# Where VectorE's side work stands in a queue: halves of x and slices of w_out behind the next subtraction, an earlier read-back, one fence a visit

## The chip, the cores and the metric

The kernel runs on one core of one Trainium2 chip. Its time is the device time of one execution in microseconds (us); the time before is the median of three runs. A profile of one execution gives the spans of the engines: TensorE (PE: matmuls; PEld: its weight loads), VectorE (DVE), ScalarE (ACT), GpSimd (POOL) and SyncE (SP), which issues most of the DMA transfers.

## What is computed

Two blocks, one after the other. The first is a retention layer: a state per batch and head decays and takes in the outer product of k and v at every step, and q reads it. The second is a feed-forward layer with SiLU.

```python
# 4 batches, 8 heads, 768 steps, head size 64
for t in range(S):
    state = gamma * state + einsum('bhd,bhe->bhde', k[:, :, t], v[:, :, t])
    y[:, :, t] = scale * einsum('bhd,bhde->bhe', q[:, :, t], state)
x = y.transpose(0, 2, 1, 3).reshape(3072, 512)
h = x @ w_in                       # 512 -> 2048
g = h * (1 / (1 + exp(-h)))
out = g @ w_out                    # 2048 -> 512
```

q, k and v are float32, the weights are given as float64.

## The kernel before

The steps are worked in chunks of 128. A unit is one chunk of one batch: 6 chunks by 4 batches, 24 units. Four units with the same chunk make a group c, and give 512 columns of x. A **visit** m runs three units in a pipeline: it transposes k and q of unit m, makes the scores of unit m-1 and the output y of unit m-2. TensorE's order is that of the program text; on the other engines a scheduler orders the instructions, when the program is built, and `tc.issue_after(i)` keeps an instruction behind instruction i.

```python
    def visit(m):
        first, mid, last = (0 <= m - i < len(units) for i in range(3))
        if first:
            stage_t(m)                       # transposes of k and q, copied by ScalarE to kt and qt
        if last:
            scores, states_with, yp = stage_y(m - 2)
            scores()                         # y from the masked scores
        if mid:
            sc, sums = score_tile(m - 1)
            stage_s(m - 1, sums)
        if last:
            states_with(0)                   # y from the states, part 0
        if mid:
            stage_a(m - 1, sc)
            with tc.issue_after(taken_out[0]) if taken_out else ExitStack():
                finish_a(m - 1, sc, sums)    # VectorE: mask, mid, state
            scale_q(m - 1)
        # ... (constants in visit 0)
        if first:
            scale_k(m)
        if last:
            states_with(1)                   # part 1
            finish_y(m - 2, yp)              # y becomes x
        # ... (loads of later k, q, v)
```

Matrix products of float32 are made of three products of parts: x is split into a high part, a low part and a mixture, and so are the weights. y lies in the PSUM tile `yp`, of which there is one, until the low half is taken:

```python
    def split_x(c, b, y, raw):
        # ... xh, xl: views of xt[c] for block b
        held[:] = [nc.scalar.activation(out=xh, in_=y, func=AF.Copy, scale=HALF).ins]
        nc.vector.tensor_tensor(out=xl, in0=y, in1=xh.bitcast(FP32), op=ALU.subtract)
        nc.vector.scalar_tensor_tensor(out=x[2], in0=x[1].bitcast(FP32), scalar=-1.0 / EPS,
                                       in1=x[0].bitcast(FP32), op0=ALU.mult, op1=ALU.add)

    LATE = 2

    def late_x(b):
        if b == 0:
            xt[LATE] = xpool.tile([128, 3, KIN, NT], FP32R, tag="xt", name=f"xt_{LATE}")
        y = hpool.tile([128, KIN, C], FP32, tag="hs", name=f"yr_{b}")
        nc.sync.dma_start(out=y, in_=y_dram[b])
        split_x(LATE, b, None, y)
```

The x of group 2 is made once into the place of the last four w_in slices, and a second time, from y kept in DRAM, for its last four products (`late_x`).

A **product** (c, f) is 12 matmuls of 128x512: eight into the PSUM bank `ha`, four into `hb`. ScalarE copies ha, VectorE subtracts hb, ScalarE applies SiLU, and g goes to DRAM. `turn` hands out three banks in rotation, to ha, hb and the transposed k of a visit.

```python
    def turn(name):
        turns[0] += 1
        return ps_h.tile([128, 512], FP32, tag=f"h{turns[0] % 3}", name=name)

    def product_in(c, f):
        ha, hb = turn(f"ha_{c}_{f}"), turn(f"hb_{c}_{f}")
        for i in range(3):
            for kk in range(KIN):
                nc.tensor.matmul(hb if i == 2 else ha, ...)
        hs = hpool.tile([128, NT], FP32, tag="hs", name=f"g_{c}_{f}")
        nc.scalar.activation(out=hs, in_=ha, func=AF.Copy, scale=ONE_E)
        taken_out[:] = [nc.vector.tensor_tensor(out=hs, in0=hs, in1=hb, op=ALU.subtract).ins]
        nc.scalar.activation(out=hs, in_=hs, func=AF.Silu)
        pending.append((c, f, hs))
```

The weights come as float64 and are turned into float32, a slice of 128 rows or columns at a time: one operation on ScalarE and six on VectorE (`convert_w`, called by `take_w`). A slice of w_in is then split into its three parts; a slice of w_out is stored in DRAM and read and split in group 5 (`w_out`). The result `cw` of a slice of w_out has one buffer.

```python
        with tc.issue_after(evac[0]) if evac else ExitStack():
            nc.scalar.activation(out=a.bitcast(FP32), in_=hi.bitcast(FP32), func=AF.Abs, scale=65536.0)
        nc.vector.tensor_scalar(out=s, ...)              # cs, L194
        nc.vector.tensor_scalar(out=a.bitcast(FP32), ...)  # ca, L196
        nc.vector.scalar_tensor_tensor(out=s, ...)       # cs, L199
        nc.vector.tensor_scalar(out=p, ...)              # cp, L201
        nc.vector.scalar_tensor_tensor(out=p.bitcast(FP32), ...)  # cp, L203
        nc.vector.tensor_tensor(out=w, ...)              # cw, L206
```

The order of the products, where a slice is taken, and which visit stands behind which product:

```python
    pairs = [(c, f) for f in range(4) for c in range(2)]
    three = [x for f in range(4, half) for x in ((0, f), (1, f), (2, f - 4))]
    rest = ([(2, f) for f in range(half - 4, NF - 4)] +
            [(c, f) for c in range(2) for f in range(half, NF - 4)])
    last = [(c, f) for c in range(3) for f in range(NF - 4, NF)]
    groups = [(c, f) for c in range(3, NC) for f in range(NF)]
    steps = pairs + three + rest + last + groups          # NF = 16, half = 8, NC = 6
    # takes: see the diff
    behind = {(1, f): lambda f=f: visit(EARLY + 2 + f) for f in range(4)}   # EARLY = 8
    at = ([(1, NF - 1)] + [(2, f) for f in range(NF - 4, NF - 1)] +
          [(c, 4 * i + 1) for c in range(3, NC - 1) for i in range(B)])
    for i, x in enumerate(at):
        behind[x] = lambda m=EARLY + 6 + i: visit(m)
```

A fence is a small memset on GpSimd that waits for one matmul and is waited for by another. It stands twice in a visit, ahead of each part of the states, because matmuls on different rows of the array would otherwise add to one PSUM bank at the same time.

Of the kernel before, what the change touches and what calls it, by code (L numbers as in the profile page):

```python
# [25 lines left out]
EPS = 2.0 ** -12  # L26
HALF = 1.0 - 2.0 ** -13
ONE_E = 1.0 + EPS
# [3 lines left out]
def kernel(  # L32
# [40 lines left out]
    scale = 1.0 / math.sqrt(D)  # L73
# [12 lines left out]
    one = pool("one", 1)  # L86
# [60 lines left out]

    staged = {}  # L150

    def load_w(i):
        if i >= 2 * NF:
            return
        if wide:
            t = stage.tile([128, 2 * DM], U32, tag="wf", name=f"wf_{i}")
            w_in, w_out, n = moe_w_in.bitcast(U32), moe_w_out.bitcast(U32), 256
        else:
            t = stage.tile([128, DM], FP32, tag="wf", name=f"wf_{i}")
            w_in, w_out, n = moe_w_in, moe_w_out, 128  # L160
        if i < NF:
            to = t.rearrange("p (i o f) -> o p i f", o=2, f=n)
            src = w_in[:, ts(i, n)].rearrange("(i o p) f -> o p i f", o=2, p=128)
            nc.sync.dma_start(out=to[0], in_=src[0])
            for j in range(2):
                nc.sync.dma_start(out=to[1, ts(j, D)], in_=src[1, ts(1 - j, D)])
        else:
            nc.sync.dma_start(out=t, in_=w_out[ts(i - NF, 128), :])
        staged[i] = t

    def convert_w(i):

        if i + W_AHEAD not in staged:
            load_w(i + W_AHEAD)
        t = staged.pop(i)
        if not wide:
            return t
        words = t.rearrange("p (c w) -> p c w", w=2)
        lo, hi = words[:, :, 0], words[:, :, 1]
        a = conv.tile([128, DM], U32, tag="ca", name=f"ca_{i}")
        s = conv.tile([128, DM], U32, tag="cs", name=f"cs_{i}")
        p = conv.tile([128, DM], U32, tag="cp", name=f"cp_{i}")  # L190
        with tc.issue_after(evac[0]) if evac else ExitStack():
            nc.scalar.activation(out=a.bitcast(FP32), in_=hi.bitcast(FP32), func=AF.Abs,
                                 scale=65536.0)
        nc.vector.tensor_scalar(out=s, in0=hi, scalar1=0x80000000, scalar2=None,  # L194
                                op0=ALU.bitwise_and)
        nc.vector.tensor_scalar(out=a.bitcast(FP32), in0=a.bitcast(FP32),  # L196
                                scalar1=bits(1024 << 20), scalar2=bits((1279 << 20) - 1),
                                op0=ALU.max, op1=ALU.min)
# [7 lines left out]
        nc.vector.tensor_tensor(out=w, in0=s.bitcast(FP32), in1=p.bitcast(FP32), op=ALU.add)  # L206
        return w
# [1 line left out]
    evac, held, w_sb = [], [], {}  # L209
    taken = [0]  # L210

    def take_w(between=lambda: None):
        i = taken[0]
        taken[0] += 1
        if i >= 2 * NF:
            return
        w32 = convert_w(i)
        between()
        if i < NF:
            w_sb[i] = split_w(i, w32, "wi", scale)  # L220
        else:
            nc.sync.dma_start(out=wo_dram[i - NF], in_=w32)
# [56 lines left out]


    xt, kt, qt, am = {}, {}, {}, {}
    taken_out = []
    state, steps_of = {}, {}


# [91 lines left out]
    def stage_y(n):  # L377

        vs, amn, qtn = kqv["v"].pop(n), am.pop(n), qt.pop(n)
        states = steps_of.pop(n)  # L380
        yp = banks("y", f"y_{n}")[:, :, : 4 * D].rearrange("p o (a t) -> p o a t", a=HP)

        started, done, new = set(), [], []

        def product(a, o, j, lhsT, rhs):
            e = j ^ (a % 2)
            i = nc.tensor.matmul(yp[ts(e, D), o, a, :], lhsT=lhsT, rhs=rhs,  # L387
                                 start=(e, o) not in started, stop=True,
                                 skip_group_check=True).ins
# [12 lines left out]
        def states_with(part):  # L402
            new.append(part)
            for a in range(HP):
                o = part ^ (a % 2)
                for j in range(2):
                    if states[o] is not None:
                        product(a, o, j, states[o][ts(j, D), a, :], qtn[ts(j, D), a, ts(o, D)])

        return scores, states_with, yp  # L410
# [15 lines left out]
    def split_x(c, b, y, raw):  # L426
        x = [xt[c][:, i, :, ts(b, C)] for i in range(3)]
        if raw is None:
            xh, xl = (t.rearrange("p a (o t) -> p o a t", o=2) for t in x[:2])
        else:  # L430
            (xh, xl), y = x[:2], raw
        held[:] = [nc.scalar.activation(out=xh, in_=y, func=AF.Copy, scale=HALF).ins]
        nc.vector.tensor_tensor(out=xl, in0=y, in1=xh.bitcast(FP32), op=ALU.subtract)  # L433
        nc.vector.scalar_tensor_tensor(out=x[2], in0=x[1].bitcast(FP32), scalar=-1.0 / EPS,
                                       in1=x[0].bitcast(FP32), op0=ALU.mult, op1=ALU.add)

    LATE = 2

    def late_x(b):
        if b == 0:
            xt[LATE] = xpool.tile([128, 3, KIN, NT], FP32R, tag="xt", name=f"xt_{LATE}")
        y = hpool.tile([128, KIN, C], FP32, tag="hs", name=f"yr_{b}")
        nc.sync.dma_start(out=y, in_=y_dram[b])
        split_x(LATE, b, None, y)

    def visit(m):

# [35 lines left out]
                nc.tensor.matmul(hb if i == 2 else ha, lhsT=w_sb[f][:, i, ts(kk, 128)],  # L485
                                 rhs=xt[c][:, i, kk, :], start=kk == 0 and i != 1,
                                 stop=kk == KIN - 1 and i != 0)
        hs = hpool.tile([128, NT], FP32, tag="hs", name=f"g_{c}_{f}")
        nc.scalar.activation(out=hs, in_=ha, func=AF.Copy, scale=ONE_E)  # L489
        taken_out[:] = [nc.vector.tensor_tensor(out=hs, in0=hs, in1=hb, op=ALU.subtract).ins]  # L490
        nc.scalar.activation(out=hs, in_=hs, func=AF.Silu)  # L491
        pending.append((c, f, hs))

# [64 lines left out]
    groups = [(c, f) for c in range(3, NC) for f in range(NF)]  # L558
    steps = pairs + three + rest + last + groups
    takes = [(0, f) for f in range(half)]  # L560
    takes += [(2, half), (2, half + 1)]
    takes += [(0, half), (0, half + 2), (1, half), (1, half + 2)]
    takes += [x for x in (last + groups)[::3]][:NF]
    behind = {(1, f): lambda f=f: visit(EARLY + 2 + f) for f in range(4)}
    at = ([(1, NF - 1)] + [(2, f) for f in range(NF - 4, NF - 1)] +
          [(c, 4 * i + 1) for c in range(3, NC - 1) for i in range(B)])
    for i, x in enumerate(at):
        behind[x] = lambda m=EARLY + 6 + i: visit(m)
    for i, bs in enumerate(((0, 1), (2,), (3,))):
        behind[1, NF - 4 + i] = lambda bs=bs: [late_x(b) for b in bs]  # L570
    for n, (c, f) in enumerate(steps):
        product_in(c, f)
        if (c, f) in takes:
            take_w()
        put_g(1)
        behind.get((c, f), lambda: None)()
        if c == NC - 1:
            if f == 0:
                get_w(0)
                get_w(1)  # L580
            if f < NF - 4:
# [68 lines left out]
```

## Time and profile before

| | |
|---|---|
| time, median of 3 runs (range) | 659.12 us (659.02 to 660.37) |
| span of the profiled execution | 655.4 us, granted TensorE clock 0.988 |
| busy: TensorE, its weight loads | 617.1 us (94%), 509.2 us (78%) |
| busy: VectorE, ScalarE, GpSimd | 428.5 us (65%), 288.1 us (44%), 14.9 us (2%) |

The busy time by stage, in us:

| stage | from to | TensorE | VectorE | ScalarE |
|---|---|---|---|---|
| visits 0 to 9, first slices of w_in | 0 to 55 | 37.3 | 38.4 | 28.5 |
| first ten products, visits 10 to 13 | 55 to 104 | 43.3 | 44.5 | 28.9 |
| products of groups 0 to 2, no visit | 104 to 186 | 82.0 | 67.5 | 53.7 |
| products with visits 14 to 25 | 186 to 339 | 143.3 | 110.7 | 71.4 |
| rest of the products with w_in | 339 to 388 | 49.0 | 33.8 | 36.4 |
| products with w_out | 388 to 655 | 262.2 | 133.7 | 69.2 |

Matmuls overlap each other, so a busy TensorE may still be slower than at its best; gaps are read from the start times in the timeline. Line numbers such as L490 are those of the kernel before; a DVE line "g<-g,hb" is the subtraction of a product.

### The profile page before, as it was taken

The page shows a single profiled execution, that of the slowest core. Times are in us where ns is not written, and L with a number is a line of the kernel's source. Part 1 is how long each engine was busy: PE and PEld are TensorE (multiplying, and loading weights), DVE is VectorE, ACT ScalarE, POOL GpSimd, SP SyncE. Part 2 cuts the span into 40 slices and gives each one's busy share as a digit, 9 for nine tenths or more (in the row PEclk, how much of TensorE's full clock was granted, in tenths as well). Part 3 has the DMA queues.
Part 4 walks back from the last instruction along what each step waited for, and adds up shares of the span by engine and source line. Part 5 has one row for each costly group of instructions (what it writes and reads, how often), then busy time and mean ns, then how long its engine had stood idle before and what let it go on. Part 6 is the DMA issues. An engine that isn't in the chain of part 4 may idle for free.

```text
span 655.4 us, 13531 instructions
## 1 busy us (share of the span) xinstructions
PE 617.1 (94%) x5440; PEld 509.2 (78%) x5440; DVE 428.5 (65%) x736; ACT 288.1 (44%) x522; POOL 14.9 (2%) x94
## 2 busy tenths in 40 slices
PE   4788889999999899999989999999999999999996
PEld 3676777888877687888768888888888888888885
DVE  2898989967968867658948856545463645454631
ACT  4546566756645444454437972222231412222311
POOL 3100000000000000000000000000000000000000
PEclk9998989999999999999999999999999999999999
DMA  9996775553577866767736654343242433433301
GB/s 196 211 209 153 198 199 179 185 171 127 192 242 170 235 178 162 226 170 237 240 113 225 202 169 127 100 159 101 92 163 95 147 110 98 159 99 95 129 0 64
DMA packets 123070, 103.64 MB, mean 158 GB/s; under 512 B 80000, under 2 KB 88192, under 8 KB 123008
## 3 DMA queue, kind: packets, MB, share of 16 engines
q1 hardware_dynamic: 119552, 96.49, 50.9%
q10 hardware_dynamic: 3456, 6.29, 2.6%
q8 instruction: 42, 0.69, 0.5%
q14 instruction: 20, 0.16, 0.1%
HBM read 66.06 MB, written 36.70 MB: 157 GB/s over the span
## 4 chain that ended last, share of the span: by engine, by line
PE 70%; DVE 17%; ACT 4%; DMA 3%; issue 3%; SPq 2%; ACTq 0%; DVEq 0%; POOL 0%; POOLq 0%
PE ha L485 18%; PE hb L485 9%; PE ob L612 7%; PE o L610 7%; PE oa L610 7%; PE o L611 7%; PE o L612 7%; PE oa L611 7%; SPq L144 2%; DVE cp L203 2%; DVE g L490 2%; DVE xt L433 2%; DVE cs L199 2%; PE y L387 1%; DVE am L363 1%
## 5 line engine op out<-in xcount | busy, mean ns | idle before, releaser
L485 PE MATMUL ha<-xt,wi 128*128 128x512 f32 x768 | 194.2, 395 | 6.0 <-DVE g L490 4.3
L485 PEld LDWEIGHTS ha<-xt,wi 128*128 128x128 f32 x768 | 142.6, 188 | 40.3 <-DVE g L490 8.3
L536 DVE TENSOR_TENSOR gs<-gr,gs 128x512 fp32r<-128x512 f32 x96 | 62.1, 685 | 90.3 <-ACT gs L534 90.3
L534 ACT ACTIVATE gs<-gr 128x512 fp32r<-128x512 f32 x96 | 53.5, 621 | 134.2 <-issue 131.8
L485 PE MATMUL hb<-xt,wi 128*128 128x512 f32 x384 | 103.0, 390 | 1.2 <-ACT g L489 1.1
L491 ACT ACTIVATE g<-g 128x512 f32<-128x512 f32 x96 | 60.6, 631 | 78.4 <-DVE g L490 78.2
L490 DVE TENSOR_TENSOR g<-g,hb 128x512 f32<-128x512 f32 x96 | 65.5, 682 | 44.4 <-PE hb L485 33.8
L485 PEld LDWEIGHTS hb<-xt,wi 128*128 128x128 f32 x384 | 71.9, 188 | 17.1 <-ACT g L489 1.6
L612 PE MATMUL ob<-wo,gs 128*128 128x512 f32 x192 | 75.3, 392 | 0.0
L610 PE MATMUL o<-wo,gs 128*128 128x512 f32 x192 | 74.7, 389 | 0.0
L610 PE MATMUL oa<-wo,gs 128*128 128x512 f32 x192 | 74.7, 389 | 0.0
L611 PE MATMUL o<-wo,gs 128*128 128x512 f32 x192 | 74.7, 389 | 0.0
L612 PE MATMUL o<-wo,gs 128*128 128x512 f32 x192 | 74.7, 389 | 0.0
L611 PE MATMUL oa<-wo,gs 128*128 128x512 f32 x192 | 74.7, 389 | 0.0
L489 ACT ACTIVATE g<-ha 128x512 f32<-128x512 f32 x96 | 56.6, 590 | 24.9 <-PE ha L485 20.1
L537 DVE SCALAR_TENSOR_TENSOR gs<-gs 128x512 fp32r<-128x512 f32 x96 | 61.9, 682 | 0.0
L612 PEld LDWEIGHTS ob<-wo,gs 128*128 128x128 f32 x192 | 36.0, 188 | 8.8 <-DVE o L618 1.5
L611 PEld LDWEIGHTS o<-wo,gs 128*128 128x128 f32 x192 | 36.0, 188 | 7.5
L612 PEld LDWEIGHTS o<-wo,gs 128*128 128x128 f32 x192 | 36.0, 188 | 7.5
L610 PEld LDWEIGHTS oa<-wo,gs 128*128 128x128 f32 x192 | 36.0, 188 | 7.5
L611 PEld LDWEIGHTS oa<-wo,gs 128*128 128x128 f32 x192 | 36.0, 188 | 7.5
L610 PEld LDWEIGHTS o<-wo,gs 128*128 128x128 f32 x192 | 36.0, 188 | 7.3
(80 smaller groups left out, 653.7 us busy)
## 6 DMA issues: line engine op xcount, KB each, us to landing
gd<-g SPq DMA_DIRECT2D x96, 256.0 KB, 2.9
gr<-gd SPq DMA_DIRECT2D x96, 256.0 KB, 2.7
wf<-in_moe_w_out_dram SPq DMA_DIRECT2D x16, 512.0 KB, 4.2
out_dram<-o ACTq DMA_DIRECT2D x24, 256.0 KB, 2.1
wf<-in_moe_w_in_dram SPq DMA_DIRECT2D x16, 256.0 KB, 3.2
wf<-in_moe_w_in_dram SPq DMA_DIRECT2D x32, 128.0 KB, 3.8
kf<-in_k_dram SPq DMA_DIRECT2D x16, 256.0 KB, 5.1
qf<-in_q_dram SPq DMA_DIRECT2D x16, 256.0 KB, 4.4
```

The lines of the kernel that those rows point to most:

```text
L144: nc.sync.dma_start(out=t, in_=src[b, :, ds(c * C, C)].rearrange("h t d -> t h d"))
L199: nc.vector.scalar_tensor_tensor(out=s, in0=a, scalar=3, in1=s, op0=ALU.logical_shift_left, op1=ALU.bitwise_or)
L485: nc.tensor.matmul(hb if i == 2 else ha, lhsT=w_sb[f][:, i, ts(kk, 128)], rhs=xt[c][:, i, kk, :], start=kk == 0 and i != 1, stop=kk == KIN ...
L489: nc.scalar.activation(out=hs, in_=ha, func=AF.Copy, scale=ONE_E)
L490: taken_out[:] = [nc.vector.tensor_tensor(out=hs, in0=hs, in1=hb, op=ALU.subtract).ins]
L491: nc.scalar.activation(out=hs, in_=hs, func=AF.Silu)
L534: nc.scalar.activation(out=t[:, 0, :], in_=g, func=AF.Copy, scale=HALF)
L536: nc.vector.tensor_tensor(out=t[:, 1, :], in0=g, in1=high, op=ALU.subtract)
L537: nc.vector.scalar_tensor_tensor(out=t[:, 2, :], in0=t[:, 1, :].bitcast(FP32), scalar=-1.0 / EPS, in1=high, op0=ALU.mult, op1=ALU.add)
L610: nc.tensor.matmul(oa, lhsT=gh, rhs=wo[f][:, 0, :], start=first_, stop=False)
L611: nc.tensor.matmul(oa, lhsT=glo, rhs=wo[f][:, 1, :], start=False, stop=last)
L612: nc.tensor.matmul(ob, lhsT=gm, rhs=wo[f][:, 2, :], start=first_, stop=last)
```

## The change

It changes the order of work and not the work. There are four parts.

- The two VectorE halves of x, for groups 3 to 5, are held back until the subtraction of the next product and queued behind it. The last block of group 3 is left where it was, since the next product but one reads it.
- The slices are taken at other products, and from P21 on (after `pairs + three`) queued behind the product's subtraction. The first two slices of w_out are taken before the last four of w_in. In groups 3 and 4 slices come midway between two visits, and the last ones at (4, 11) to (5, 3).
- y of group 2 is read back well ahead of its use, and three of the four blocks lie in the buffers of kt and qt instead of those of g. The second making of its x is queued behind a product's copy and subtraction.
- Part 0 of the states now uses, for each bank, the rows that the scores used, so it needs no fence; only part 1 keeps one.

```diff
+    SEQ = [*range(NF - 4), NF, NF + 1, *range(NF - 4, NF), *range(NF + 2, 2 * NF)]
...
-    def take_w(between=lambda: None):
+    def take_w(after=None):
...
-        w32 = convert_w(i)
-        between()
+        with tc.issue_after(after) if after else ExitStack():
+            w32 = convert_w(at)
+        i = SEQ[at]
...
         def states_with(part):
-            new.append(part)
+            new.extend([part] * part)
             for a in range(HP):
-                o = part ^ (a % 2)
-                for j in range(2):
+                for o in range(2):
+                    j = o ^ part
                     if states[o] is not None:
                         product(a, o, j, states[o][ts(j, D), a, :], qtn[ts(j, D), a, ts(o, D)])
...
-        nc.vector.tensor_tensor(out=xl, in0=y, in1=xh.bitcast(FP32), op=ALU.subtract)
-        nc.vector.scalar_tensor_tensor(out=x[2], ...)
+        def rest():
+            nc.vector.tensor_tensor(out=xl, in0=y, in1=xh.bitcast(FP32), op=ALU.subtract)
+            nc.vector.scalar_tensor_tensor(out=x[2], ...)
+        if c > LATE and (c, b) != (LATE + 1, B - 1):
+            behind_next.append(rest)
+        else:
+            rest()
...
+    def late_y(b):
+        p, tag, bufs = ((one, "kt", 2), (one, "qt", 3), (hpool, "hs", 3), (one, "kt", 2))[b]
+        y_late[b] = p.tile([128, KIN, C], FP32, tag=tag, name=f"yr_{b}", bufs=bufs)
+        nc.sync.dma_start(out=y_late[b], in_=y_dram[b])
+
     def late_x(b):
...
-        y = hpool.tile([128, KIN, C], FP32, tag="hs", name=f"yr_{b}")
-        nc.sync.dma_start(out=y, in_=y_dram[b])
-        split_x(LATE, b, None, y)
+        with tc.issue_after(copied[0]), tc.issue_after(taken_out[0]):
+            split_x(LATE, b, None, y_late.pop(b))
...
         taken_out[:] = [nc.vector.tensor_tensor(out=hs, in0=hs, in1=hb, op=ALU.subtract).ins]
+        with tc.issue_after(taken_out[0]):
+            while behind_next:
+                behind_next.pop()()
...
     takes = [(0, f) for f in range(half)]
-    takes += [(2, half), (2, half + 1)]
+    takes += [(2, half - 4), (2, half - 2)]
+    takes += [(2, half), (2, half + 2)]
     takes += [(0, half), (0, half + 2), (1, half), (1, half + 2)]
-    takes += [x for x in (last + groups)[::3]][:NF]
+    takes += [(0, NF - 4), (0, NF - 2)]
+    takes += [(3, f) for f in (3, 7, 11, 15)] + [(4, f) for f in (3, 7, 11, 12, 14, 15)]
+    takes += [(5, 0), (5, 3)]
...
-    for i, bs in enumerate(((0, 1), (2,), (3,))):
-        behind[1, NF - 4 + i] = lambda bs=bs: [late_x(b) for b in bs]
+    behind[0, NF - 2] = lambda: [late_y(b) for b in range(2)]
+    behind[1, NF - 4] = lambda: [late_y(2), late_x(0), late_x(1)]
+    behind[1, NF - 3] = lambda: [late_y(3), late_x(2)]
+    behind[1, NF - 2] = lambda: late_x(3)
...
-            take_w()
+            take_w(taken_out[0] if n >= len(pairs + three) else None)
```

More of the change, by code (lines that the diff above doesn't have):

```diff
@@ L145, in load, with load_w @@
         kqv[name][n] = t
+    SEQ = [*range(NF - 4), NF, NF + 1, *range(NF - 4, NF), *range(NF + 2, 2 * NF)]
     staged = {}
-    def load_w(i):
-        if i >= 2 * NF:
+    def load_w(at):
+        if at >= 2 * NF:
             return
+        i = SEQ[at]
         if wide:
@@ L168, in load_w, with convert_w @@
             nc.sync.dma_start(out=t, in_=w_out[ts(i - NF, 128), :])
[L169 to L183, printed above, removed]
+        staged[at] = t
+    def convert_w(at):
+        if at + W_AHEAD not in staged:
+            load_w(at + W_AHEAD)
+        t, i = staged.pop(at), SEQ[at]
         if not wide:
@@ L210 @@
     taken = [0]
-    def take_w(between=lambda: None):
-        i = taken[0]
+    def take_w(after=None):
+        at = taken[0]
         taken[0] += 1
-        if i >= 2 * NF:
+        if at >= 2 * NF:
             return
-        w32 = convert_w(i)
-        between()
+        with tc.issue_after(after) if after else ExitStack():
+            w32 = convert_w(at)
+        i = SEQ[at]
         if i < NF:
@@ L281 @@
     xt, kt, qt, am = {}, {}, {}, {}
-    taken_out = []
+    behind_next = []
+    taken_out, copied = [], []
     state, steps_of = {}, {}
@@ L432, in split_x @@
         held[:] = [nc.scalar.activation(out=xh, in_=y, func=AF.Copy, scale=HALF).ins]
-        nc.vector.tensor_tensor(out=xl, in0=y, in1=xh.bitcast(FP32), op=ALU.subtract)
-        nc.vector.scalar_tensor_tensor(out=x[2], in0=x[1].bitcast(FP32), scalar=-1.0 / EPS,
-                                       in1=x[0].bitcast(FP32), op0=ALU.mult, op1=ALU.add)
-    LATE = 2
+        def rest():
+            nc.vector.tensor_tensor(out=xl, in0=y, in1=xh.bitcast(FP32), op=ALU.subtract)
+            nc.vector.scalar_tensor_tensor(out=x[2], in0=x[1].bitcast(FP32),
+                                           scalar=-1.0 / EPS, in1=x[0].bitcast(FP32),
+                                           op0=ALU.mult, op1=ALU.add)
+        if c > LATE and (c, b) != (LATE + 1, B - 1):
+            behind_next.append(rest)
+        else:
+            rest()
+    LATE = 2
+    y_late = {}
+    def late_y(b):
+        p, tag, bufs = ((one, "kt", 2), (one, "qt", 3), (hpool, "hs", 3), (one, "kt", 2))[b]
+        y_late[b] = p.tile([128, KIN, C], FP32, tag=tag, name=f"yr_{b}", bufs=bufs)
+        nc.sync.dma_start(out=y_late[b], in_=y_dram[b])
     def late_x(b):
@@ L488, in product_in @@
         hs = hpool.tile([128, NT], FP32, tag="hs", name=f"g_{c}_{f}")
-        nc.scalar.activation(out=hs, in_=ha, func=AF.Copy, scale=ONE_E)
+        copied[:] = [nc.scalar.activation(out=hs, in_=ha, func=AF.Copy, scale=ONE_E).ins]
         taken_out[:] = [nc.vector.tensor_tensor(out=hs, in0=hs, in1=hb, op=ALU.subtract).ins]
+        with tc.issue_after(taken_out[0]):
+            while behind_next:
+                behind_next.pop()()
         nc.scalar.activation(out=hs, in_=hs, func=AF.Silu)
```

## The prediction

> **What bounds the kernel now.** I read the page's busy slices first, then TensorE's waits, then the timeline of TensorE from product to product, and last VectorE's timeline in front of one late product.
>
> ```profile
> PE   4788889999999899999989999999999999999996
> DVE  2898989967968867658948856545463645454631
> PEclk9998989999999999999999999999999999999999
> ```
>
> Each digit is a 16.4 us slice. TensorE is full from slice 8 on, but for slices 12, 14 and 21; VectorE is nearly full only in the first eight. The second half (388 to 655 us, the product with w_out) is solid: 1152 matmuls at 0.227 us are 261 us. So the question is what TensorE loses before 388 us, and to whom:
>
> ```profile
> PE ha L485 <- DVE g L490: 4.3, 7, 1.5
> PE kp L329 <- DVE g L490: 4.1, 2, 2.1
> PE y L387 <- DVE xt L433: 2.5, 1, 2.5
> PE ha L485 <- DVE xt L433: 1.4, 1, 1.4
> PE hb L485 <- ACT g L489: 1.1, 1, 1.1
> PE y L387 <- POOL token L303: 0.6, 2, 0.3
> ```
>
> Columns are total us, times, longest. The releasers are VectorE's subtraction (L490), its halves of x (L433), and hardly the fence (L303). This view undercounts, because part of each wait lies at the weight load. I therefore take start-to-start times of the 96 products in the timeline (P1 to P96 in the order of `steps`). An undisturbed product takes 2.72 us, the first after a visit 2.86, a visit 3.11. What is above that is lost: P41 0.36, P43 1.42, visit 16 (after P46) 2.6, P49 2.09, and in groups 3 and 4 P52 0.29, P56 1.15, P60 0.29, P64 0.47, P68 0.44, P72 0.44, P76 1.70 (sum 4.78). Earlier: P6 2.23, P8 2.22, visit 10 1.1, visit 13 1.5, P1 and P10 0.8 each. From P11 to P40 and from P79 on nothing is lost.
>
> P56 shows the mechanism. VectorE between two subtractions:
>
> ```profile
> 247.57 0.69 DVE L490 TENSOR_TENSOR g<-g,hb 128x512 f32<-128x512 f32 x1 [1.69 <-PE hb L485]
> 248.18 0.68 DVE L313 TENSOR_TENSOR kf<-kf,gk 128x512 f32<-128x512 f32 x1
> 250.16 0.43 DVE L196 TENSOR_SCALAR ca<-ca 128x512 f32<-128x512 f32 x1 [1.30 <-ACT ca L192]
> ...
> 254.62 0.68 DVE L433 TENSOR_TENSOR xt<-y,xt 128x512 fp32r<-128x512 f32 x1
> 255.22 0.68 DVE L206 TENSOR_TENSOR cw<-cs,cp 128x512 f32<-128x512 f32 x1
> 255.81 0.68 DVE L434 SCALAR_TENSOR_TENSOR xt<-xt 128x512 fp32r<-128x512 f32 x1
> 256.42 0.68 DVE L490 TENSOR_TENSOR g<-g,hb 128x512 f32<-128x512 f32 x1
> ```
>
> The product P55 ended at about 253.3, but its subtraction started at 256.42: a slice of w_out (L196 to L206), the visit's operations and both halves of x stood ahead of it. And TensorE:
>
> ```profile
> 255.09 1.07 PE L485 MATMUL hb<-xt,wi 128*128 128x512 f32 x4
> 257.15 1.20 PE L485 MATMUL ha<-xt,wi 128*128 128x512 f32 x4 [0.99 <-DVE g L490]
> ```
>
> P57 starts 0.05 after that subtraction ends. The three rotating banks explain it: ha of product n+2 takes the bank of hb of product n. So a subtraction, normally done 0.94 us after its product ends (start at +0.25, 0.69 long), may be 1.7 us late and no more.
>
> **What the skill says.** "PSUM — Partial Sum Buffer", section "Engine vs sequencer instructions": the queues of ScalarE and VectorE are strictly first in, first out. The trace agrees: the subtraction at 256.42 had its input 2.9 us earlier. The same page, "PSUM bank collisions raise a hardware error": two TensorE writes from different row tiles into one bank and quadrant collide. That is why there is a fence; no run so far shows the collision. "VectorE: DVE Perf Modes", "Two Vector instructions with no wait between them": an instruction that is not held starts before the one in front has finished. The trace agrees: 0.68 us operations start 0.60 apart when independent, 0.72 when dependent. I use those spacings (0.33 for the 0.42 ones). "DMA: Bandwidth & Descriptors", "Anatomy of one DMA": about 2 us fixed plus bytes at 436 GB/s, so 2.6 us for 256 KB, an estimate; the trace has 2.7 to 2.9 for g and y, but 3.9 for the slices' stores, which I use.
>
> **The change part by part.** No arithmetic is added or removed. The instruction order of the two built programs is the same on VectorE up to the subtraction of P17, so P1 to P10 lose what they lost (8.7 us stay).
>
> *Slices.* In groups 3 and 4 a visit stands behind every fourth product, and slices came every third. Now they come after the second product behind a visit. With V the start of a visit, VectorE has k's scaling at V+1.1, the mask, two state sums and q's scaling from V+2.95 to V+4.8; the first product ends at V+6.0, its subtraction runs V+6.2 to 6.9, the halves of x to V+8.2; the second ends at V+8.7, is subtracted by 9.6, and the slice's first five operations take until V+12.2; the third ends at V+11.4, is subtracted by 12.9 where 14.1 would do. Nothing is late, so all 4.78 us go.
>
> *Halves of x.* After P45 to P47 a visit follows at once. The low half reads y from PSUM, and there is one y tile. It now waits for the next subtraction (+0.25), comes at +0.85 and ends at +1.53; the next visit wants y at +0.96. So visits 15, 16 and 17 wait about 0.6 each, 1.85, where before they lost 2.7: a gain of 0.85. The last block of group 3 is exempt and no slice stands before it: x is complete before P49 needs it, and 2.09 goes.
>
> *Read-back of group 2.* y comes from DRAM long before, two blocks outside the g buffers. P41's and P43's 1.78 go. But VectorE then has a slice's end and four operations between the subtractions of P41 and P42: 5 x 0.60, so P42's ends about 1.8 after its product where 2.66 is the limit.
>
> *Fence.* In a full visit the other matmuls already cover it (16 of them take 0.47 to 0.49). It shows only at visit 25, 0.30 + 0.29, and at visit 9, where GpSimd is busy with gq until 52.95. I count 0.6.
>
> *New costs.* The last six slices go to products (4,11) to (5,3), where nothing was lost before, and meet the splits of the first four g tiles. There VectorE has alternately 3.06 and 2.13 us of work per product of 2.72, so the lag grows by 0.3 to 0.5 and shrinks again, inside 1.7. The slices' 512 KB loads (4.2 us) and the one cw buffer (store 3.9 us) are tighter: I put 1.0 for them, and 0.6 for the same cw wait before P42. These are estimates from the trace's landing times.
>
> Sum: 4.78 + 0.85 + 2.09 + 1.78 + 0.6 = 10.1 gained, 1.6 given back: 8.5 us. From 659.1 that is 650.6.
>
> **Rivals.** (a) Group 5 becomes VectorE-bound. From (4,14) to (5,15) its work is 17 subtractions, four slices (3.3 each), two halves of x, four splits (1.2 each) and ten w_out slices (1.2 each), 17 x 0.6 + 13.2 + 1.2 + 4.8 + 12 = 41 in 46 us. That is against it, but any wait for a load there has little room. It would give back 3 to 5: 653 to 655. (b) The y tile costs more than 0.6 a visit, since the halves stand behind a subtraction that may itself be late: 1.5 x 3 makes 653. (c) The fence is worth more than I think: if each of the 16 visits between products got 0.2 shorter, 647.5. Against it: in the visits the state matmuls start where the covering matmuls end. (d) Off-path only: the late subtractions were hidden. Against it: each late product is released within 0.06 of a subtraction.
>
> **Range and chances.** Everything within reach of the change sums to about 12 us, so 647 is nearly a floor; waits in group 5 and at y could return half. 80%: 647 to 654. Faster by over 2% (under 645.9) would need more than all: 0.04. Slower by over 2%: 0.01. Within: 0.95.
>
> **What would show it.** In the changed profile P52, P56, P60, P64, P68, P72 and P76 take 2.72; VectorE's halves of x come right after a subtraction; TensorE's wait on xt's low half appears three times, 0.6 each, at visits 15 to 17; P41, P43 and P49 take 2.72 to 2.9; products of group 5 show at most 1 us of waits; slices 1 to 6 and the last 267 us are unchanged. I am wrong if group 5 shows several waits on the subtraction, if a store of cw holds VectorE before P42, or if the early products change.

## The result and the profile after

| | before | after |
|---|---|---|
| time, median (range), runs side by side | 659.07 us (656.44 to 660.37) | 650.56 us (648.75 to 651.8) |
| span of the profiled execution | 655.4 us | 647.8 us |
| granted TensorE clock in it | 0.988 | 1.000 |
| busy: TensorE, VectorE, ScalarE | 617.1, 428.5, 288.1 us | 612.7, 427.5, 289.1 us |

The ratio is 0.9874, with a 95% interval of 0.9835 to 0.9912: 8.5 us less. The total is the predicted one. Its parts are not, and the rest of this text is about them.

The page of the changed kernel, busy tenths in slices of 16.2 us:

```profile
PE   5787989999998899999999999999999999999996
DVE  2799989678986656665689787455463635464631
PEclk9999999999999999999999999999999999999999
```

Slice 21 of TensorE is full now. What is left, but for the first six, is in slices 13 and 14, from 194 to 227 us. The clock row is clean in this execution, while that of before has two eights.

TensorE's waits in the changed kernel (total us, times, longest):

```profile
PE kp L334 <- DVE g L511: 3.5, 2, 2.1
PE y L392 <- issue: 3.4, 4, 1.7
PE ha L506 <- issue: 2.2, 2, 1.8
...
PE y L392 <- DVE xt L441: 2.0, 3, 0.7
...
PE ha L506 <- DVE g L511: 1.2, 1, 1.2
PE hb L506 <- ACT g L510: 1.0, 1, 1.0
PE y L392 <- POOL token L308: 0.5, 2, 0.3
```

The wait of a product on the subtraction (now L511) has gone from 4.3 us to one of 1.2 (behind P10, where nothing was to change), and that on x's halves (1.4) has left the list of the products. The y tile is waited for three times for 0.65 to 0.66 us, where it was once for 2.5. A new one stands there: 1.8 us of "issue" in front of a product, a wait with no releaser. Of the two waits on the fence (token) one is left at visit 25 (0.30), where there were two; the other is 0.19 at visit 9.

VectorE in front of P57, the product that before stood 0.99 us:

```profile
251.06 0.69 DVE L511 TENSOR_TENSOR g<-g,hb 128x512 f32<-128x512 f32 x1 [1.31 <-ACT g L510]
251.67 0.68 DVE L441 TENSOR_TENSOR xt<-y,xt 128x512 fp32r<-128x512 f32 x1
252.39 0.69 DVE L442 SCALAR_TENSOR_TENSOR xt<-xt 128x512 fp32r<-128x512 f32 x1
253.78 0.69 DVE L511 TENSOR_TENSOR g<-g,hb 128x512 f32<-128x512 f32 x1 [0.70 <-PE hb L506]
254.39 0.42 DVE L197 TENSOR_SCALAR cs<-wf 128x512 uint32<-128x512 uint32 x1
```

Subtraction, halves of x, idle, next subtraction, and only then the slice: what the change wants. VectorE waits for TensorE here, and P57 takes 2.72.

Start-to-start times of the products by stage, from TensorE's timeline (us; every visit inside a stage is in it):

| run | P1-P10 | P11-P40 | P41-P49 | P50-P78 | P79-P95 |
|---|---|---|---|---|---|
| before | 48.97 | 81.79 | 44.29 | 108.89 | 46.38 |
| after | 49.58 | 81.73 | 43.22 | 102.09 | 46.87 |
| e1 two fences | 48.88 | 81.92 | 43.29 | 103.09 | 47.18 |
| e2 halves not queued | 49.58 | 82.58 | 39.10 | 102.22 | 49.34 |
| e3 old read-back | 49.41 | 82.51 | 50.40 | 102.23 | 47.02 |
| e4 old slices | 49.08 | 81.81 | 42.28 | 105.90 | 46.37 |
| e5 e2 + y early | 49.58 | 81.83 | 39.53 | 102.12 | 48.53 |
| e6 visit 17 exempt | 48.68 | 81.81 | 40.36 | 102.08 | 47.15 |
| e7 e2 + old slices | 49.23 | 81.78 | 40.96 | 108.42 | 46.37 |
| e8 e5 + spread slices | 50.94 | 82.09 | 39.72 | 102.09 | 46.72 |
| e9 y by GpSimd | 48.88 | 82.13 | 41.91 | 102.09 | 47.21 |
| e10 stores by GpSimd | 48.73 | 82.50 | 38.88 | 103.06 | 47.69 |
| e11 after + 4 stores moved | 51.08 | 82.36 | 43.05 | 102.07 | 46.97 |
| e12 best | 51.55 | 82.76 | 38.61 | 102.16 | 47.15 |

The change in the span (7.6 us) is 0.8 before P41, 1.1 in P41 to P49, 6.8 in P50 to P78, and 1.1 given back behind. The first column is a warning. From after to e12 no edit touches that stage but the fence of e1, yet it spreads from 48.7 to 51.6. So single totals can't decide about 1 or 2 us; the later columns can, since an undisturbed product repeats to 0.01 (2.72). Each row is one execution, though: that of e3 (657.8) is among its slowest, and that of e7 (652.37) its fastest.

The stage P41 to P49 should have gained 4.1 and gained 1.1. Three losses stand in it in the changed kernel: visits 15 to 17 with 3.78, 3.77 and 3.96 where an unhindered visit takes 3.05; P44 with 4.27; and P48 with 4.78 where 2.86 is normal. The last two were not predicted. P44 first, on ScalarE and then on SyncE's queue:

```profile
192.49 0.63 ACT L515 ACTIVATE g<-g 128x512 f32<-128x512 f32 x1 [1.79 <-DVE g L511]
194.58 0.63 ACT L438 ACTIVATE xt<-yr 128x512 fp32r<-128x512 f32 x1 [1.46 <-DMA yr<-yd]
195.34 0.60 ACT L510 ACTIVATE g<-ha 128x512 f32<-128x512 f32 x1
```

```profile
189.48 0.32 SPq L226 DMA_DIRECT2D wod<-cw  x1
189.90 0.38 SPq L461 DMA_DIRECT2D yr<-yd  x1
```

ScalarE stands 1.46 us at the third block of y read back for group 2. P43's copy of ha, which P44 needs, is queued behind it. That block was asked for at 189.90, right after the store of a w_out slice, and came 4.7 us later.

P48 on TensorE:

```profile
220.61 0.98 PE L506 MATMUL ha<-xt,wi 128*128 128x512 f32 x3
223.35 0.84 PE L506 MATMUL ha<-xt,wi 128*128 128x512 f32 x3 [1.77 <-issue]
```

Three matmuls run, then nothing for 1.77 us, and no engine or transfer is named.

### The profile page after: what moved, and what is told of

Same layout as the page of the kernel before. It is cut to its first block, busy times and chain, and to the rows that moved or that the text cites. A ratio compares the mean times of both kernels' runs of the same rounds, so it can differ in the third digit from the quotient of the medians.

```text
span 647.8 us, 13480 instructions
## 1 busy us (share of the span) xinstructions
PE 612.7 (95%) x5440; PEld 505.8 (78%) x5440; DVE 427.5 (66%) x736; ACT 289.1 (45%) x522; POOL 13.1 (2%) x70
## 5 line engine op out<-in xcount | busy, mean ns | idle before, releaser
L511 DVE TENSOR_TENSOR g<-g,hb 128x512 f32<-128x512 f32 x96 | 65.6, 684 | 41.6 <-ACT g L510 26.0
```

## The experiments

All are edits of the changed kernel, and compute the same thing. Times are medians of four or five executions (14 for e3 and e7); "lost" is what a product takes above 2.72 (2.86 behind a visit). The kernel before, run beside them, had medians of 657.8 to 658.5 us, against 659.07 beside the changed kernel, so a difference of about 1 us between a median here and the changed kernel's 650.56 means nothing.

**e1: two fences again.**

```diff
-            new.extend([part] * part)
+            new.append(part)
             for a in range(HP):
-                for o in range(2):
-                    j = o ^ part
+                o = part ^ (a % 2)
+                for j in range(2):
```

> The changed kernel with the fences of before (two a visit, states read in the old order), all else as changed. Theory (a fence is covered by the 16 other matmuls of a full visit and shows only at the last one): full visits go from 3.05 back to 3.11 us and visit 25 from 1.62 to 2.14, so about 1.2 us more: 651.8. Rival (the fence was worth 0.2 us in each of the 16 visits between products): 3 us more or above: 653.6.

650.69 us (649.91 to 651.2). Every full visit takes 3.11 instead of 3.05 and visit 25 takes 2.14 instead of 1.62, with both old token waits of 0.30 and 0.29. In the table P50 to P78 is 1.00 longer; with 0.2 in visits 15 to 17 the fence is worth about 1.2 us. The medians differ by 0.1, so the total doesn't resolve it. A fence worth 3 us falls.

**e2: halves of x not queued.**

```diff
-        if c > LATE and (c, b) != (LATE + 1, B - 1):
+        if False:
             behind_next.append(rest)
```

> The changed kernel, but the halves of x of groups 3 to 5 are not held back for the next subtraction. Theory (the slices were what made the subtractions late; the deferral only makes visits 15, 16 and 17 wait 0.65 us each for the y tile): those visits go from 3.8 to 3.1 us, P52 to P76 stay at 2.72, 2.0 us less: 648.6. Rival (the deferral is what keeps the subtractions after a visit in time): the waits of visits 15 to 17 go, but P52, P56, P60, P64, P68, P72, P76 lose 0.3 us or more each: 650.6 or above.

647.95 us (645.57 to 649.84): 2.6 below the changed kernel, or 1.6 by the two ratios to the kernel before that ran beside them (0.985 and 0.9874), and the ranges overlap; the stage P41 to P49 decides, with 4.1 less. Visits 15 to 17 take 3.05 each, P48 loses nothing, and P52 to P76 stay at 2.72. So the queueing of the halves gains nothing in groups 3 and 4 once the slices have moved, and costs 4 us at P45 to P48. It has a use elsewhere: without it group 5 loses 3.0 instead of 0.5 (above all P81 0.46, P82 0.36, P83 0.92, P87 0.39, P88 0.41). VectorE's waits from 326 to 380 us, in this run and then in the changed kernel, show one reason:

```profile
DVE wol L118 <- DMA wod<-cw: 2.6, 2, 1.6
DVE cw L209 <- DMA wod<-cw: 2.4, 1, 2.4
```

```profile
DVE wol L118 <- DMA wod<-cw: 2.8, 2, 2.0
DVE cw L209 <- DMA wod<-cw: 1.1, 1, 1.1
```

The second line of each is a slice that can't be written since the one buffer of cw is still being stored: 1.3 us longer in e2, just ahead of P81 to P83. The first lines are alike and explain nothing. The losses at P87 and P88 are not explained.

**e3: old read-back** (asked for and split at the same place, in the buffers of g):

```diff
-        with tc.issue_after(copied[0]), tc.issue_after(taken_out[0]):
-            split_x(LATE, b, None, y_late.pop(b))
+        y = hpool.tile([128, KIN, C], FP32, tag="hs", name=f"yr_{b}")
+        nc.sync.dma_start(out=y, in_=y_dram[b])
+        split_x(LATE, b, None, y)
...
-    behind[0, NF - 2] = lambda: [late_y(b) for b in range(2)]
-    behind[1, NF - 4] = lambda: [late_y(2), late_x(0), late_x(1)]
-    behind[1, NF - 3] = lambda: [late_y(3), late_x(2)]
-    behind[1, NF - 2] = lambda: late_x(3)
+    for i, bs in enumerate(((0, 1), (2,), (3,))):
+        behind[1, NF - 4 + i] = lambda bs=bs: [late_x(b) for b in bs]
```

> The changed kernel, but y of group 2 is read back as before (four blocks in the g buffers, at their use). Theory (P41 and P43 lose 1.8 us with the old read-back and P44 1.55 with the new one): P44 runs undisturbed, P42 to P43 lose 1.4 to 1.8, the time is 650.5 to 651. Rival (the early read-back is worth its 1.8 us and P44's wait comes from elsewhere): P44 still loses 1.5 and the time is 652.4.

655.03 us (652.48 to 658.13). The expectation fell: by the medians the early read-back is worth 4.5 us here, not the 1.78 that P41 and P43 lost before (7.2 in the stage P41 to P49 of the profiled execution, 1.6 of it at P48, where most matmuls start 0.43 us apart instead of 0.23). P43 alone takes 5.67 longer. ScalarE in this run:

```profile
189.83 0.63 ACT L516 ACTIVATE g<-g 128x512 f32<-128x512 f32 x1 [0.76 <-DVE g L512]
195.69 1.25 ACT L438 ACTIVATE xt<-yr 128x512 fp32r<-128x512 f32 x2 [5.22 <-DMA yr<-yd]
```

Two blocks, asked for at 190.91 behind a slice's load and a slice's store, arrive at 195.7. Before the change the slices were taken elsewhere, and P43 lost 1.42; the new places of the slices make the early read-back necessary. The parts of the change are not independent.

**e4: old slices, with the halves still queued.**

```diff
-    takes += [(2, half - 4), (2, half - 2)]
-    takes += [(2, half), (2, half + 2)]
+    takes += [(2, half), (2, half + 1)]
     takes += [(0, half), (0, half + 2), (1, half), (1, half + 2)]
-    takes += [(0, NF - 4), (0, NF - 2)]
-    takes += [(3, f) for f in (3, 7, 11, 15)] + [(4, f) for f in (3, 7, 11, 12, 14, 15)]
-    takes += [(5, 0), (5, 3)]
+    takes += [x for x in (last + groups)[::3]][:NF]
...
-            take_w(taken_out[0] if n >= len(pairs + three) else None)
+            take_w()
```

> The changed kernel, but the slices are taken where they were before and not queued behind subtractions. Theory (slices in front of the subtraction made P52 to P76 late): most of the 4.8 us come back in groups 3 and 4, group 5 loses its 0.5 us less, the time is 654.5 to 655.5. Rival (the halves of x in front of the subtraction were what made it late, and they stay behind it here): P52 to P76 stay at 2.72 and the time is under 651.5.

651.67 us (650.7 to 652.71; the edit also puts the slices back in their old order), against an expected 654.5 to 655.5. Of the 4.78 that P52 to P76 lost before, 2.75 come back (P56 0.44, P60 1.20, P72 0.29, P76 0.72). Visit 16 waits 1.76 us for the y tile. P44 and group 5 lose nothing. The slices are therefore worth about half of what I gave them, *if* the halves are queued.

**e7: neither queueing** (the edits of e2 and e4 together).

> Both queueings away: halves of x at once, slices of w_out at the old products, at once and in the old order; the earlier read-back and the single fence stay. Theory: queueing the halves and queueing the slices each spare P52 to P76 most of the same 4.8 us, so each alone could be taken away cheaply (648.0 and 651.7 us), but not both; then P52, P56, P60, P64, P68, P72, P76 lose 4 to 5 us together and the time is 654 to 655.5 us. Rival: the slices at their old products cost what they cost whatever the halves do, 2.6 us; then the sum of the losses is 2.2 to 3 us and the time 650 to 651.5.

655.28 us (652.37 to 657.42), as the theory has it. In the profiled execution, the fastest, P52 to P76 lose 5.37 together. VectorE in front of a late subtraction in this run:

```profile
249.96 0.69 DVE L441 TENSOR_TENSOR xt<-y,xt 128x512 fp32r<-128x512 f32 x1
250.56 0.68 DVE L209 TENSOR_TENSOR cw<-cs,cp 128x512 f32<-128x512 f32 x1
251.16 0.69 DVE L442 SCALAR_TENSOR_TENSOR xt<-xt 128x512 fp32r<-128x512 f32 x1
251.76 0.68 DVE L511 TENSOR_TENSOR g<-g,hb 128x512 f32<-128x512 f32 x1
```

Halves and slice stand ahead of the subtraction again, the same queue as in the kernel before. What P52 to P76 lose, in four runs:

| | slices at new products, queued | slices at old products |
|---|---|---|
| halves queued | 0.00 (after) | 2.75 (e4) |
| halves not queued | 0.00 (e2) | 5.37 (e7) |

The new treatment of the slices removes the loss by itself. Queueing the halves removes half of it by itself. They stand in for each other, and what "one of them is worth" depends on the other. No run has the slices at the new products without queueing them, so which of these two does it is not shown.

**e6: the block of visit 17 also exempt from the queueing.**

```diff
-        if c > LATE and (c, b) != (LATE + 1, B - 1):
+        if c > LATE and (c, b) not in ((LATE + 1, B - 2), (LATE + 1, B - 1)):
```

> The changed kernel with one more block of x exempt from the queueing: that of visit 17. Visits 15 and 16 still wait for their y tile. Theory: the 1.8 us that P48 lost without any wait that the profile names belong to the wait of TensorE in visit 17 just before it (instructions that follow are fetched late); then visit 17 takes 3.05 us, P48 about 2.9 us, visits 15 and 16 keep their 0.65 us waits, and the time is about 2.6 us below the changed kernel, 648.0. Rival: P48 stops at this place for a reason of its own, such as the transfers of the w_out slice and of the y pieces; then P48 keeps its 1.3 to 2.0 us and the time is about 0.8 us below, 649.8.

647.74 us (646.81 to 650.21), 2.8 less than the changed kernel (1.7 by the ratios; 2.9 in the stage P41 to P49); 2.6 was expected. Visits 15 and 16 still wait 0.66 us each, visit 17 takes 3.05, and P48's stop is gone, though the products, loads and slices around it are the same:

```profile
220.27 2.11 PE L506 MATMUL ha<-xt,wi 128*128 128x512 f32 x8
```

So P48's stop hangs on the wait in the visit before it. (The edit also moves this block's two halves on VectorE to before P48's subtraction; no wait of TensorE in P48 names them.) What the stop is, the DMA view suggests. It has a queue that carries instructions: 42 transfers of 16 KB, 0.69 MB in all. If it serves TensorE alone, that is 63 bytes for each of its 10,880 matmuls and weight loads, or some 256 of them per transfer. That queue in the changed kernel, from 220.61 to 223.35, inside P48 (packets, MB, share); in visit 17 before it (216.65 to 220.61) the queue has no line:

```profile
q8 instruction: 1, 0.02, 2.3%
```

and in e6 from 217.22 to 220.30, inside visit 17, and no line in P48:

```profile
q8 instruction: 1, 0.02, 2.6%
```

With the wait, the transfer starts 4.1 us after the visit does (220.75), ends at 221.76, and TensorE goes on at 223.35. Without it, it starts 0.4 us after the visit (217.60) and nobody notices. The four further runs that wait at visit 17 (e1, e3, e4, e11) stop in the same product, for 1.28 to 1.78 us, and there the transfer starts between 0.5 us before the visit's end and 0.3 us after it; the runs that don't wait there stop for 0.17 us at most. That the stop comes with the wait in the visit is shown.

The traces have more such stops, the kernel before too:

```profile
41.52 0.38 PE L387 MATMUL y<-am,kqv 64*64 64x64 f32 x9 [1.62 <-issue]
```

In the 14 traces TensorE stops 76 times for 0.15 us or more with no releaser named. Every one of these stops ends 1.24 to 1.80 us after a transfer of the instruction queue has ended (this one at 40.00). And counted in matmuls from the start of the program, they stand at ten places only, 127 or a multiple of 127 apart (to within 3). With their weight loads that is nearly what one 16 KB transfer holds by the estimate above. One such place lies behind P48's third matmul (its fourth in e4, its fifth in e7). So TensorE waited there for its next instructions: the places and the times leave little else, though no run changed the fetching alone. Why the wait in visit 17 makes the transfer start late is not shown.

**e5: as e2, third block of y asked for one product earlier** (the text on record says two).

```diff
-    behind[1, NF - 4] = lambda: [late_y(2), late_x(0), late_x(1)]
+    behind[0, NF - 1] = lambda: late_y(2)
+    behind[1, NF - 4] = lambda: [late_x(0), late_x(1)]
```

> The halves of x are not queued (as in the run without deferral), and the third piece of y for group 2 is asked for two products earlier, ahead of the store of the converted w_out slice instead of behind it. Theory: P44 lost 1.55 to 1.8 us because ScalarE stood at the square piece of that y, whose load had been issued behind that store; then P44 falls to about 2.8 us, P48 stays at about 2.9, the rest is as without deferral, and the time is about 646.3 us (1.6 below the 647.95 of that run). Rival: the load is not late because of its place in the queue but because of the traffic of those microseconds; then P44 still takes 4.2 to 4.5 us and the time stays at 647.5 to 648.5.

648.0 us (647.23 to 649.14). P44 is clean as expected, and the time does not move: P42 now loses 1.08 and P43 1.21. ScalarE in this run:

```profile
190.24 0.60 ACT L510 ACTIVATE g<-ha 128x512 f32<-128x512 f32 x1 [2.12 <-DMA gd<-g]
```

The block of y lies in one of the three buffers that the gates g rotate through. Held earlier, it makes the next gate wait until an older one is stored. The loss has moved.

**e8: as e5, the last twelve slices spread over groups 3 and 4.**

```diff
-    takes += [(3, f) for f in (3, 7, 11, 15)] + [(4, f) for f in (3, 7, 11, 12, 14, 15)]
-    takes += [(5, 0), (5, 3)]
+    takes += [(c, f) for c in (3, 4) for f in (2, 4, 7, 10, 12, 15)]
```

> As the run with y early and no deferral, with the last twelve w_out slices taken six to a group in groups 3 and 4 (products 2, 4, 7, 10, 12, 15 of each), none in group 5. Theory: the losses of group 5 without deferral (P81 to P88, 2.5 us) are VectorE's, which there has the slices, the last halves and the gates; without slices in group 5 they go, and nothing new waits in groups 3 and 4, where VectorE has room: about 644 us. Rival: the extra slices of groups 3 and 4 delay the mask or a product's second half, and 1.5 to 3 us come back there: 645.5 to 647.

647.41 us (646.39 to 647.65), not the expected 644. In the stages the theory holds: group 5 takes 46.72 instead of 48.53 and P50 to P78 102.09, as in the changed kernel. But its profiled execution has 50.94 in P1 to P10, in a stage it does not touch, and P42 and P43 still lose 2.5. The total can't show a gain of 1.8 against that.

**e9: as e8, but the third block of y at its place in the changed kernel, asked for by GpSimd's queue.**

```diff
-        nc.sync.dma_start(out=y_late[b], in_=y_dram[b])
+        (nc.gpsimd if b == 2 else nc.sync).dma_start(out=y_late[b], in_=y_dram[b])
```

> The run with spread slices, but the third piece of y keeps its place of the changed kernel (behind P41) and is asked for by GpSimd's queue instead of SyncE's. Theory: both losses come from order: behind the slice's store in SyncE's queue the piece is late and P44 waits (1.8 us); asked for earlier it takes one of the three tiles of the gates too soon, and P42 and P43 wait for the gate's store (1.1 and 1.4 us). In a queue of its own it is neither: P42, P43 and P44 take 2.7 to 2.9 us each and the time is about 2.4 us below the 647.4 of the run before, 645.0. Rival: the three tiles are too few for a fourth user at any place, or the memory traffic of those microseconds makes every transfer slow: then 1 us or more stays on P42 to P45 and the time is 646.3 to 647.5.

648.22 us (646.0 to 648.97). The theory fell. P44 loses 3.60. On GpSimd and on ScalarE:

```profile
189.78 0.71 POOL L461 DMA_DIRECT2D yr<-yd  x1 [95.84 <-DMA gd<-g]
```

```profile
195.62 0.63 ACT L438 ACTIVATE xt<-yr 128x512 fp32r<-128x512 f32 x1 [5.28 <-DMA yr<-yd]
```

In a queue of its own the load starts no sooner (189.78; 189.90 in the changed kernel), since it waits for a gate's store to free its buffer, and it takes 5.8 us. In the changed kernel that store landed at 189.31, so the place behind the slice's store cost the load 0.6 us at most.

**e10: as e8, y as in the changed kernel, all stores of w_out slices asked for by GpSimd. e11: the changed kernel with only its first four stores moved so. e12: as e10, but only the first four.** The edit of e11 and e12 (e10 has `nc.gpsimd` for all):

```diff
-            nc.sync.dma_start(out=wo_dram[i - NF], in_=w32)
+            (nc.gpsimd if i < NF + 4 else nc.sync).dma_start(out=wo_dram[i - NF], in_=w32)
```

> The run with spread slices, the y pieces as in the changed kernel on SyncE's queue, but the stores of the converted w_out slices are asked for by GpSimd. Theory: what made the third piece of y late was SyncE standing at that store until the slice was converted; without it P42 to P44 take 2.7 to 2.9 us each, and the time is about 645.0. Rival: GpSimd now stands at the stores in its turn, and its token for the fence of a visit comes late: visits with a store just before them lose 0.5 to 1 us, six or more of them, and the time is 647 to 650.

> The changed kernel with one thing moved: the stores of its first four converted w_out slices (those taken at the products of groups 0 to 2) are asked for by GpSimd's queue, so that SyncE doesn't stand at them ahead of the third piece of y. Theory: P44's 1.55 us come from the store ahead of that load; the load is asked for 1.3 us sooner and P44 takes 3.0 us or less, with up to 1.1 us going to P42 as in the run with all stores moved; the sum of the losses of P42 to P44 is 1.6 us at most, P48 keeps its 1.3 to 2.0 us, and the time is 650 us, within half a us of the changed kernel. Rival: the third piece is late because its transfer takes 5 us whenever it is asked for; then P44 still loses 1.3 us or more.

> The run with all stores moved, but only the first four stores on GpSimd's queue, the other twelve on SyncE's. Theory: the mask and token waits of visits 19, 21 and 23 (0.3 us each) and the 0.97 us that P50 to P78 lost in that run were GpSimd standing at the stores; they go, P50 to P78 take 102.1 us again and P41 to P49 stay at 38.9: about 645.5 us. Rival: those waits do not come from the stores and stay: 646.8 us.

e10: 646.81 us (646.11 to 647.74). P44 loses 0.24, P42 1.13. The rival has its share: visits 19, 21 and 23 take 0.3 more, two of them with a token wait of 0.16.

e11: 650.3 us (650.08 to 651.07), its profile near the theory's numbers: P42 loses 1.22, P43 0.28, P44 0.16, P48 1.67. But the reason I gave is not borne out: the block is asked for 4.6 us after P41's start, against 5.0 before. P44 is clean largely because P42 has already waited, now for a store on VectorE:

```profile
191.49 0.69 DVE L209 TENSOR_TENSOR cw<-cs,cp 128x512 f32<-128x512 f32 x1 [2.22 <-DMA wod<-cw]
```

e12: 645.91 us (644.48 to 648.05), ratio 0.9822 (0.9796 to 0.9848): the lowest median, 4.6 below the changed kernel (3.4 by the ratios). It can't be told apart from e10, whose ratio is 0.9816 (0.9791 to 0.9841). The waits of visits 19 to 23 are gone (P50 to P78 102.16) and P41 to P49 are the shortest, 38.61. It differs from the changed kernel in three things: no queueing of the halves, slices spread and none in group 5, four stores on GpSimd.

## Why the prediction was right in total and wrong in parts

The prediction's 8.5 us are 4.1 for P41 to P49, 5.4 for groups 3 and 4 (slices and visit 25's fence), and 1.0 given back in group 5.

*Slices (4.78).* Right: P52 to P76 take 2.72, and the timeline has the predicted order. The run of e2 adds that the halves' queueing was not needed for it, and that of e4 that with the slices at their old places 2.0 of the 4.78 go as well. In all, P50 to P78 gained 6.8: 4.78, then 1.1 in products behind the late ones (a late product also delayed its successor's start a little, 0.15 here and there, which I had not counted), and 0.9 of the fence.

*Halves of x (0.85).* The mechanism and the size of the waits were right: 0.6 predicted three times, 0.65, 0.66 and 0.66 measured. Half of the step failed: I took the three waits as the whole price. The wait of visit 17 also makes P48 stop, 1.9 us above its normal 2.86, so the part lost about 1.6 instead of gaining 0.85 (visits 15 to 17: 2.7 above 3.11 before, 2.4 above 3.05 after; P48: 1.9 more). So rival (b), a y tile that costs more than 0.6 a visit, came in another form. In the profile before nothing stops at P48, where visit 16 waited and not 17, but three stops of the same kind (1.62, 0.66 and 0.91 us) stand in its first 65 us, and the prediction has no such cost. P49's 2.09 went as predicted.

*Read-back (1.78).* P41 and P43 went to 2.72 as predicted. The step that failed is "y comes from DRAM long before". It is true of two blocks, asked for at 102.02 and 104.20. The third, in a gate's buffer, was asked for only at 189.90 and landed 4.7 us later, and cost P44 1.55. I had 0.6 in the sum for a wait at P42, on the store of cw. That wait did not occur in the changed kernel; it occurred in e11. The prediction took 2.7 to 2.9 us for such a load from the trace before; here 4.2 to 5.8 us were measured. The cause is in the traces: a slice at its new place brings its 512 KB load into the same microseconds (187.97 to 193.30 in the changed kernel). While the third block was on its way, from 189.90 to 194.60, the data queue took this share of the 16 DMA engines (packets, MB, share):

```profile
q1 hardware_dynamic: 728, 1.54, 95.3%
```

Of all read-backs behind the start of P41, in the 14 traces, the 17 that share 2.2 us or more with such a load took 4.2 to 5.8 us, and the 15 that share 1.1 us or less 2.7 to 3.8. With the slices at their old places (e4, e7) the third block took 3.2 and 2.9 us and P44 lost nothing. The shortage is of buffers and of transfers, not of order: e5 and e11 each relieve one wait and find another, and e9 only lengthens the old one (1.7 to 3.6 us lost in P42 to P44 each time).

*Fence (0.6).* About 1.2: 0.5 at visit 25, and 0.06 in every full visit, which I had taken as covered. The 0.6 was the sum of both waits at visit 25, but one fence stays there and still waits 0.30; that 0.5 came all the same is luck in this step.

*Group 5 (1.0 given back).* 0.5. Rival (a) did not come, but it was close: e2, which leaves the halves where they were, loses 3.0 there.

So P41 to P49 fell short by 3.0, and that was made up: 1.4 more in P50 to P78, 0.5 less in group 5, and 0.8 before P41, less than that part varies between kernels that are alike there (P41 starts at 184.9 us in the changed kernel, and between 184.4 and 187.0 in e2, e5, e6, e8 and e9); against these stand 0.6 behind P95, which I had at none. The profiled spans differ by 7.6, the medians by 8.5; that the total was met is luck, by errors that cancel and by what the executions vary. Two readings of the prediction are wrong and nothing rests on them: TensorE's row has a 9 in slice 12, and (4, 11), one of the products "where nothing was lost before", is P76, which lost 1.70.

## What to carry to other kernels

When two edits take work out of the same queue ahead of the same instruction, their gains don't add; measure them in a two-by-two before keeping both, since one may only bring its own price (here 4 us at three visits and the product behind them, for a gain that the other had already made). Before moving a load earlier, ask which buffer it lands in, what frees that buffer, and which other transfers run then: in e9 a queue of its own didn't help a load that waited for a buffer. Judge small gains by the start-to-start times of one stage; the total carries the luck of other stages.

## What was not expected of the hardware

A wait of 0.66 us inside TensorE's stream was followed, 3 us and some 260 matmuls and weight loads later, by a stop of 1.28 to 1.78 us that no engine explains, in five kernels out of five that had the wait there; the nine without it stop for 0.17 us at most. Such stops come at fixed places, about every 127 matmuls where they come at all, and end 1.24 to 1.80 us after a 16 KB transfer of the instruction queue (76 of 76). In the changed kernel that transfer came 4.1 us after the visit's start, in e6 0.4. The same wait in the two visits before had no such consequence. In P1 to P10 such stops take 0.91 us before and 2.70 after, more than the stage's whole difference of 0.6. And read-backs of 256 KB took 4.2 to 5.8 us where a slice's 512 KB load ran beside them, against 2.7 to 3.8 where it did not.
